# Attention and SwiGLU FFN on one core: a reordered ramp, a set FFN pace, and batch 1 loaded in natural layout

## The chip, the core, the metric

The kernel runs on one core of a Trainium2 chip. Times are device microseconds (us). A profile is one profiled execution; its span is a little shorter than the timed run. One slot is the work on one pair of heads; a batch has four. TensorE is called PE, VectorE DVE, ScalarE ACT, GpSimd POOL, SyncE SP. In the views, `st` and `X` are the PSUM banks (the memory that matmuls write) of scores and of values, `f` those of the FFN and of transposes, `PT` the exponentials, `XN` the attention output, `XS` and `XT` its normalized copy before and after transposition. The granted clock is the share of TensorE's full clock: 1.00 is full, 0.50 half.

## The reference

Block-causal attention over q, k, v of shape (8 batches, 8 heads, 576 tokens, 64), blocks of 64; its output is laid out as 4608 tokens of 512, and a gated FFN follows:

```python
scores = q @ k.T / 8;  scores = where(block_i >= block_j, scores, -1e9)
x = softmax(scores) @ v                       # -> x[b * 576 + s, h * 64 + d]
xn = x / sqrt(mean(x * x) + 1e-6) * rms_g
out = (silu(xn @ w_gate) * (xn @ w_val)) @ w_out      # 512 -> 1536 -> 512
```

## The kernel before

All loads are issued by POOL, which casts float32 to bfloat16 on the way. Batches 0 and 1 are loaded "wide": six tokens to a partition, so one run in memory is 1536 B, and TensorE transposes them. Batches 2 to 7 are loaded in natural layout (256 B runs) and transposed by DMA.

```python
def load_wide(b, n, h0, h1):                   # 96 partitions, 6 tokens of 64 each
    pool_dma(out=wide[b][:, n, hs, :, :]..., in_=(q, k)[n][b, hs, :, :].rearrange("h (p s) d -> p h (s d)", s=SLOT))
def load_qk_head(b, h):                        # natural: two loads for each head
    pool_dma(out=t[:, hp, kb:kb + NC, ds], in_=k[b, h, 0:TAIL, :].rearrange("(c p) d -> p c d", p=P))
    pool_dma(out=t[:, hp, 0:NC, ds], in_=q[b, h, 0:TAIL, :]...)
def prep(b, hp):                               # DMA transpose, issued by SP
    sp(nc.sync.dma_start_transpose(out=T, in_=QKN[b % 2][:, hp, :, :]))
```

A slot is made of pieces: three score groups of the current pair (each followed by an exp on ACT) and two values groups of the previous pair (probabilities times V, then an eviction on DVE into `XN`). After each piece a share of the queued FFN work runs, so that PE has something to do while ACT works. FFN work is counted in units of one 512-wide matmul; gate, value and down groups are 4 units each. A chunk of tokens joins the queue when its attention is done and normalized: `norm_squares` on ACT, a reciprocal root in small DVE steps, `XS` on DVE, transposes on PE, `XT` on ACT.

```python
for n in range(3):
    pieces.append(cur.scores(n))
    if n < 2: pieces.append(prev.values(n))
...
fast = b == 0
at(norms, s0, norm_squares(b));  at(norms, s0 + (0 if fast else 1), norm_scale(b))
s1 = s0 + (1 if fast else 2);    at(norms, s1, xt_by_pe(b)); at(rels, s1, release(b))
...
budget = max(0, total - RESERVE) / (nxt - s)   # units for this slot
```

(Shortened. In slot 4, the first of batch 1, this kernel already puts both values pieces ahead of the scores.)

The softmax here doesn't subtract the row's maximum and nothing guards it: scores larger than these inputs give would overflow.

Of the kernel before, what the change touches and what calls it, by code (L numbers as in the profile page):

```python
# [11 lines left out]
BF16 = mybir.dt.bfloat16  # L12
AF = mybir.ActivationFunctionType
# [4 lines left out]
def kernel(  # L18
# [11 lines left out]
    nc = tc.nc  # L30
# [19 lines left out]
    const = ctx.enter_context(tc.tile_pool(name="const", bufs=1))  # L50
    tp = ctx.enter_context(tc.tile_pool(name="tp", bufs=3))
    xtp = ctx.enter_context(tc.tile_pool(name="xtp", bufs=3))
# [27 lines left out]
    def pool(ins):  # L80
        return chain("POOL", ins)
# [18 lines left out]
    PTS = [const.tile([P, PTW], BF16, name=f"PT{i}") for i in range(2)]  # L100
    QK0 = [const.tile([P, 2, S], BF16, name=f"QK0{i}") for i in range(2 * HP)]
    ident = const.tile([P, P], BF16, name="ident")
# [4 lines left out]
    wide = []  # L107
    for b in range(2):
        t = hbuf.tile([P, NMC, BANK], BF16, name="HT")
        wide.append(t[0:PQ, :, :].rearrange("p m q -> p (m q)")[:, 0:2 * H * SLOT * D].rearrange(  # L110
            "p (n h s d) -> p n h s d", n=2, h=H, s=SLOT))
    WIDE = 2

# [58 lines left out]
    def tpose_wide(b, hp):  # L172
        T = QK0[b * HP + hp]
        for n in range(2):
            t = fbank().bitcast(BF16)
            for s in range(SLOT):
                for par in range(2):
                    pe(nc.tensor.transpose(t[par * D:(par + 1) * D, s * PQ:(s + 1) * PQ],
                                           wide[b][:, n, 2 * hp + par, s, :],
                                           ident[0:PQ, 0:PQ]))  # L180
            nc.vector.tensor_copy(out=T[:, n, :].rearrange("p (j s) -> p j s", s=SLOT),
                                  in_=t[:, 0:S].rearrange("p (s j) -> p j s", s=SLOT))
        tposed[b, hp] = T[:, 0, :], T[:, 1, :]
# [21 lines left out]
    class Pair:  # L205
# [18 lines left out]
        def scores(self, n, split=None):  # L224
# [3 lines left out]
            end = 0  # L228
            tail = self.full and n == 2
            for c, lo, w, o in self.groups[n]:  # L230
# [6 lines left out]
            if tail:  # L237
                for h in range(2):
                    self.qk(XB[h][:, BANK - BLK:BANK], h, NC, TAIL, BLK)
                    self.col[h, NC, NC] = 3 * T4 + h * BLK  # L240
            if split:
# [11 lines left out]
            if tail:  # L253
                for h in range(2):
                    a = 3 * T4 + h * BLK
                    nc.scalar.activation(out=PT[:, a:a + BLK], in_=XB[h][:, BANK - BLK:BANK],
                                         func=AF.Exp, scale=SM_SCALE)
            for tn, o, step, cnt in self.diags:
# [63 lines left out]
    def norm_scale(b, tiles):  # L322
        XN = xn_tiles[b]
        n = len(tiles)
        XS = xs.tile([P, n, DM], BF16, name="XS")

        def root():
            norm_tiles[b, tiles[0], "rs"] = inv_sqrt(norm_tiles.pop((b, tiles[0])), n)
            norm_tiles[b, tiles[0]] = XS

        def one(j, t):
            rs = norm_tiles[b, tiles[0], "rs"]
            nc.vector.tensor_scalar(out=XS[:, j, :], in0=XN[:, t, :],  # L333
                                    scalar1=rs[:, j:j + 1], scalar2=None, op0=ALU.mult)
        return [root] + [lambda j=j, t=t: one(j, t) for j, t in enumerate(tiles)]
# [49 lines left out]
    def up_gate(i, k):  # L385
        pg, _ = up_tile(i, k)
        th = act.tile([P, BANK], FP32, name="th")
        nc.scalar.activation(out=th, in_=pg, func=AF.Tanh, scale=0.5)  # L388
        nc.vector.scalar_tensor_tensor(out=th, in0=th, scalar=1.0, in1=pg,  # L389
                                       op0=ALU.add, op1=ALU.mult)  # L390
        gates[i, k] = th

    def up_val(i, k):
        pv, ht = up_tile(i, k)
        nc.vector.tensor_tensor(out=ht, in0=gates.pop((i, k)), in1=pv, op=ALU.mult)  # L395

    outs = {}

    def down(i, s, part):
# [6 lines left out]
        if part == 2:  # L406
# [3 lines left out]
            sp(nc.sync.dma_start(out=out[r0:r0 + P, :], in_=ob))  # L410

    def add_chunk(i):
        n = (chunks[i][1] - chunks[i][0]) // P
        for k in range(NMC * n // 4):
            queue.append((4, lambda k=k: up_gate(i, k)))
            queue.append((4, lambda k=k: up_val(i, k)))
        for s in range(n):
            for part in range(3):
                queue.append((4, lambda s=s, part=part: down(i, s, part)))

# [9 lines left out]


    load_wide(0, 0, 0, 2)
    load_wide(0, 1, 0, 2)
    make_identity(nc, ident)
    load_wide(0, 0, 2, 4)
    load_wide(0, 1, 2, 4)
    load_v_chunk(0, 0)
    load_v_chunk(0, 1)
    load_wide(0, 0, 4, H)
    load_wide(0, 1, 4, H)  # L440
    load_v_chunk(0, 2)
# [9 lines left out]
    for m in range(0, NMC, 3):  # L451
        load_up_weights(m, m + 3)
    for n in range(2):
        load_wide(1, n, 0, H)
    for c in range(NC):
# [7 lines left out]
    early = [Pair(0, hp, EARLY) for hp in range(HP)]  # L463
    for hp in range(HP):
        tpose_wide(0, hp)
        early[hp].scores(0, (None, FB[0:2], FB[2:4])[hp % 3])
        if hp > 1:
            early[hp - 2].values(0)
    early[2].values(0)
    early[3].values(0)  # L470
    clear_v(1)
# [18 lines left out]
    for b in range(B):  # L490
        tiles = T1 if b == 0 else TA
        s0 = index[b, HP - 1] + 1
        fast = b == 0
        at(norms, s0, lambda b=b, tiles=tiles: norm_squares(b, tiles))
# [5 lines left out]
    e0 = index[1, 0]  # L500
    mids = {e0 + i: lambda i=i: tpose_wide(1, i + 1) for i in range(HP - 1)}
    for b in range(WIDE, B):
        for hp in range(HP):
            at(preps, index[b, hp] - 2, lambda b=b, hp=hp: prep(b, hp))
    for b in range(WIDE, B):
        s0 = max(index[b - 2, HP - 1] - 1, e0)
        s1 = index[b, 0] - 2
        if b > WIDE:
            at(loads, s0, lambda b=b: load_qk_tail(b))
            for h in range(H):  # L510
                at(loads, s0 + h * (s1 - s0) // H, lambda b=b, h=h: load_qk_head(b, h))
# [4 lines left out]

    RESERVE = 12
    prev = None
    for s, sl in enumerate(slots):
        todo = [g for f in norms.pop(s, []) for g in f()]  # L520
        nxt = min([r for r in ready if r > s] + [999])
        total = sum(c for c, _ in queue)
        budget = max(0, total - RESERVE) / (nxt - s) if nxt < 999 else total / (len(slots) - s)
        cur = None
# [7 lines left out]
        for n in range(3):  # L532
            pieces.append((lambda n=n: cur.scores(n)) if cur else None)
            if n < 2:
                pieces.append((lambda n=n: prev.values(n)) if prev else None)
        if s == e0:
            tpose_wide(1, 0)
            pieces = [pieces[1], pieces[3], pieces[0], pieces[2], pieces[4]]
        left = 0
        for i, f in enumerate(pieces):  # L540
            if f:
                f()
            if i == 2 and s in mids:
                mids[s]()
            if i == 3 and s > e0:
# [40 lines left out]
```

## Time and profile before

| | before |
|---|---|
| median of the first 3 runs | 414.1 us |
| profiled span | 412.1 us |
| PE busy | 379.6 us (92%) |
| PE idle in 0 to 100 us, in 100 to 380, after | 26.0, 2.7, 3.7 us |
| time of a batch once PE is full | 41.78 us |

The table says where to look: PE is full after the first quarter, so every step is judged by when the ramp ends and whether the full stretch stays full. The lines are in the prediction below.

### The profile page before, as it was taken

The page shows a single profiled execution, that of the slowest core. Times are in us where ns is not written, and L with a number is a line of the kernel's source. Part 1 is how long each engine was busy: PE and PEld are TensorE (multiplying, and loading weights), DVE is VectorE, ACT ScalarE, POOL GpSimd, SP SyncE. Part 2 cuts the span into 40 slices and gives each one's busy share as a digit, 9 for nine tenths or more (in the row PEclk, how much of TensorE's full clock was granted, in tenths as well). Part 3 has the DMA queues.
Part 4 walks back from the last instruction along what each step waited for, and adds up shares of the span by engine and source line. Part 5 has one row for each costly group of instructions (what it writes and reads, how often), then busy time and mean ns, then how long its engine had stood idle before and what let it go on. Part 6 is the DMA issues. An engine that isn't in the chain of part 4 may idle for free.

```text
span 412.1 us, 7988 instructions
## 1 busy us (share of the span) xinstructions
PE 379.6 (92%) x3096; PEld 193.4 (47%) x3096; DVE 249.4 (61%) x652; ACT 235.5 (57%) x451; POOL 134.0 (33%) x184
## 2 busy tenths in 40 slices
PE   3469779887999999999999999999999999999996
PEld 2337545664444544454445444544454444444442
DVE  5455864673779276926692669267926872752760
ACT  2276756786585758576757575757674625322321
POOL 8643497886079006910691060000000000000000
PEclk9999998999999999999999999999999999999999
DMA  9999999999299639972998397231020002002002
GB/s 99 190 203 186 169 89 169 131 149 130 61 107 117 105 76 102 110 128 68 83 125 130 70 79 69 86 81 35 0 78 27 0 27 76 1 2 102 1 2 102
DMA packets 140950, 36.70 MB, mean 89 GB/s; under 512 B 127600, under 2 KB 136304, under 8 KB 140912
## 3 DMA queue, kind: packets, MB, share of 16 engines
q0 software_dynamic: 103712, 18.89, 56.8%
q1 hardware_dynamic: 37200, 17.31, 18.4%
q8 instruction: 24, 0.39, 0.4%
q14 instruction: 14, 0.11, 0.1%
HBM read 37.75 MB, written 9.44 MB: 115 GB/s over the span
## 4 chain that ended last, share of the span: by engine, by line
PE 75%; DVE 12%; ACT 7%; DMA 2%; issue 2%; POOL 1%; ACTq 0%; POOLq 0%; DVEq 0%
PE f_91 L87 19%; PE f_89 L87 15%; PE f_88 L87 15%; PE f_90 L87 12%; PE st L87 6%; PE X_86 L87 3%; PE X_87 L87 3%; DVE HT L395 2%; DVE th L389 2%; DVE XS L333 2%; DMA HT<-in_k_dram 2%; ACT th L388 2%; DVE XN L284 2%; ACT sq L318 2%; ACT PT_96 L246 1%
## 5 line engine op out<-in xcount | busy, mean ns | idle before, releaser
L87 PEld LDWEIGHTS <-WV 128*128 128x128 bf16 x480 | 43.5, 98 | 45.9 <-issue 6.9
L87 PEld LDWEIGHTS <-WG 128*128 128x128 bf16 x480 | 43.5, 98 | 42.9 <-issue 4.3
L87 PEld LDWEIGHTS <-HT 128*128 128x128 bf16 x432 | 38.6, 98 | 47.3 <-issue 9.6
L389 DVE SCALAR_TENSOR_TENSOR th<-th,f_88 128x512 f32<-128x512 f32 x53 | 36.4, 686 | 40.3 <-ACT th L388 39.9
L87 PE MATMUL f_90<-XT,WG 128*128 128x512 bf16 (+1 forms) x248 | 56.7, 356 | 0.0
L87 PE MATMUL f_91<-XT,WV 128*128 128x512 bf16 (+1 forms) x240 | 55.7, 358 | 0.0
L87 PE MATMUL f_89<-XT,WV 128*128 128x512 bf16 (+1 forms) x240 | 55.7, 358 | 0.0
L87 PE MATMUL f_88<-XT,WG 128*128 128x512 bf16 (+1 forms) x232 | 55.4, 366 | 0.0
L388 ACT ACTIVATE th<-f_88 128x512 f32<-128x512 f32 x53 | 31.9, 603 | 40.3 <-PE f_88 L87 39.2
L246 ACT ACTIVATE PT_96<-st 128x1024 bf16<-128x1024 f32 x44 | 45.1, 1024 | 16.2 <-PE st L87 16.2
L246 ACT ACTIVATE PT_97<-st 128x1024 bf16<-128x1024 f32 x44 | 45.7, 1038 | 11.4 <-PE X_87 L87 6.6
L87 PE MATMUL f_91<-WO,HT 128*128 128x512 bf16 x192 | 48.2, 384 | 2.1 <-ACT ob L408 2.1
L389 DVE SCALAR_TENSOR_TENSOR th<-th,f_90 128x512 f32<-128x512 f32 x55 | 37.7, 686 | 19.0 <-ACT th L388 18.9
L388 ACT ACTIVATE th<-f_90 128x512 f32<-128x512 f32 x55 | 33.1, 601 | 27.6 <-PE f_90 L87 24.6
L395 DVE TENSOR_TENSOR HT<-th,f_89 128x512 bf16<-128x512 f32 x54 | 37.1, 687 | 5.6 <-PE f_89 L87 1.6
L395 DVE TENSOR_TENSOR HT<-th,f_91 128x512 bf16<-128x512 f32 x54 | 37.1, 686 | 3.6
L78 POOL DMA_DIRECT2D VN_95<-in_v_dram x20 | 17.1, 874 | 51.6 <-PE X_87 L87 45.7
L87 PE MATMUL st<-QKT 64*128 64x512 bf16 (+4 forms) x240 | 28.2, 297 | 2.2 <-ACT PT_97 L246 1.6
L78 POOL DMA_DIRECT2D VN_94<-in_v_dram x20 | 17.1, 906 | 36.6 <-PE X_87 L87 36.6
L87 PE MATMUL f_88<-WO,HT 128*128 128x512 bf16 x108 | 26.2, 380 | 0.2 <-DVE HT L395 0.2
L78 POOL DMA_DIRECT2D QKN_92<-in_k_dram x30 | 23.0, 766 | 8.9 <-DMA QKT<-QKN_92 3.4
L318 ACT ACTIVATE sq<-XN 128x512 bf16<-128x512 f32 x40 | 25.6, 639 | 0.1
(126 smaller groups left out, 475.5 us busy)
## 6 DMA issues: line engine op xcount, KB each, us to landing
out_dram<-ob SPq DMA_DIRECT2D x36, 256.0 KB, 2.0
VN_94<-in_v_dram POOLq DMA_DIRECT2D x16, 128.0 KB, 4.8
VN_95<-in_v_dram POOLq DMA_DIRECT2D x16, 128.0 KB, 4.7
WG<-in_moe_w_gate_dram POOLq DMA_DIRECT2D x4, 384.0 KB, 10.8
WV<-in_moe_w_val_dram POOLq DMA_DIRECT2D x4, 384.0 KB, 11.7
WO<-in_moe_w_out_dram POOLq DMA_DIRECT2D x2, 768.0 KB, 14.0
QKN_92<-in_k_dram POOLq DMA_DIRECT2D x24, 64.0 KB, 3.5
QKN_92<-in_q_dram POOLq DMA_DIRECT2D x24, 64.0 KB, 3.6
```

The costliest lines, as they stand in the source:

```text
L78: return chain("POOL", nc.gpsimd.dma_start(**kw))
L87: pe(nc.tensor.matmul(dst, w, r, start=start, stop=stop))
L246: nc.scalar.activation(out=PT[:, a0:a0 + T4], in_=ST, func=AF.Exp, scale=SM_SCALE)
L284: nc.vector.tensor_tensor(out=xn_tiles[self.b][:, t0:t0 + n, f0:f0 + m * D].rearrange("p t (h d) -> p h t d", h=m), in0=xv[:, :, :, 0:D], ...
L318: nc.scalar.activation(out=sq, in_=XN[:, t, :], func=AF.Square, accum_out=ss[:, j:j + 1])
L333: nc.vector.tensor_scalar(out=XS[:, j, :], in0=XN[:, t, :], scalar1=rs[:, j:j + 1], scalar2=None, op0=ALU.mult)
L388: nc.scalar.activation(out=th, in_=pg, func=AF.Tanh, scale=0.5)
L389: nc.vector.scalar_tensor_tensor(out=th, in0=th, scalar=1.0, in1=pg, op0=ALU.add, op1=ALU.mult)
L395: nc.vector.tensor_tensor(out=ht, in0=gates.pop((i, k)), in1=pv, op=ALU.mult)
```

## The change

The intent is to shorten the ramp. Q and K of batch 0 are loaded ahead of its V and the transposes of all its pairs are issued together; the FFN units of slots 2 to 9 are set by a table; batch 1 is loaded and transposed as later batches are, which spares TensorE 96 transposes. Around this, the pieces are reordered, the last small score block of both heads shares one PSUM bank, batch 1 is normalized one slot earlier, some DVE instructions get a fixed order, and chunk 0's down groups wait for chunk 1. Smaller edits come along that no run takes apart: the identity matrix is built in place, `tp` has a fourth buffer, and slot 4 loses its own order. The diff is shortened and reworded to fit.

```diff
+            copy = nc.scalar.copy if b == 0 and n == 1 else nc.vector.tensor_copy   # tpose_wide
-            tail = self.full and n == 2       # both heads, banks X0 and X1
+            tail = self.full and n > 0        # head 1 at n=1, head 0 at n=2, both in bank X0
-            nc.vector.tensor_scalar(out=XS...        # and th, HT
+            chain("DVE", nc.vector.tensor_scalar(out=XS...
+    later = []                                # down groups of chunk 0 wait for chunk 1
-    load_v_chunk(0, 0); load_v_chunk(0, 1)    # then Q, K of heads 4 to 7
+    for h in range(4, H, 2): load_wide(0, 0, h, h + 2); load_wide(0, 1, h, h + 2)
+    load_v_chunk(0, 0); load_v_chunk(0, 1)
-    for n in range(2): load_wide(1, n, 0, H)
+    load_qk_tail(1)
+    for h in range(H): load_qk_head(1, h)
-        tpose_wide(0, hp); early[hp].scores(0, ...); early[hp - 2].values(0)   # in turn
+    tpose_wide(0, 0); tpose_wide(0, 1); early[0].scores(0); tpose_wide(0, 2) ...
+    for pr in early: pr.values(0)
-        fast = b == 0
+        fast = b < 2
+    PACE = {2: 24, 3: 24, 4: 12, 5: 12, 6: 12, 7: 12, 8: 22, 9: 22}
-            pieces.append(scores(n)); if n < 2: pieces.append(values(n))
+            if n < 2: pieces.append(values(n)); pieces.append(scores(n))
```

More of the change, by code (lines that the diff above doesn't have):

```diff
@@ L6 @@
 from concourse import bass_utils, mybir
-from concourse.masks import make_identity
 from concourse._compat import with_exitstack
@@ L50 @@
     const = ctx.enter_context(tc.tile_pool(name="const", bufs=1))
-    tp = ctx.enter_context(tc.tile_pool(name="tp", bufs=3))
+    tp = ctx.enter_context(tc.tile_pool(name="tp", bufs=4))
     xtp = ctx.enter_context(tc.tile_pool(name="xtp", bufs=3))
@@ L100 @@
     PTS = [const.tile([P, PTW], BF16, name=f"PT{i}") for i in range(2)]
-    QK0 = [const.tile([P, 2, S], BF16, name=f"QK0{i}") for i in range(2 * HP)]
+    QK0 = [const.tile([P, 2, S], BF16, name=f"QK0{i}") for i in range(HP)]
     ident = const.tile([P, P], BF16, name="ident")
@@ L107 @@
     wide = []
-    for b in range(2):
-        t = hbuf.tile([P, NMC, BANK], BF16, name="HT")
-        wide.append(t[0:PQ, :, :].rearrange("p m q -> p (m q)")[:, 0:2 * H * SLOT * D].rearrange(
+    wide.append(hbuf.tile([P, NMC, BANK], BF16, name="HT")[0:PQ, :, :].rearrange(
+        "p m q -> p (m q)")[:, 0:2 * H * SLOT * D].rearrange(
             "p (n h s d) -> p n h s d", n=2, h=H, s=SLOT))
-    WIDE = 2
+    WIDE = 1
     def load_wide(b, n, h0, h1):
@@ L180, in tpose_wide @@
                                            ident[0:PQ, 0:PQ]))
-            nc.vector.tensor_copy(out=T[:, n, :].rearrange("p (j s) -> p j s", s=SLOT),
-                                  in_=t[:, 0:S].rearrange("p (s j) -> p j s", s=SLOT))
+            copy = nc.scalar.copy if b == 0 and n == 1 else nc.vector.tensor_copy
+            copy(out=T[:, n, :].rearrange("p (j s) -> p j s", s=SLOT),
+                 in_=t[:, 0:S].rearrange("p (s j) -> p j s", s=SLOT))
         tposed[b, hp] = T[:, 0, :], T[:, 1, :]
@@ L237, in scores @@
             if tail:
-                for h in range(2):
-                    self.qk(XB[h][:, BANK - BLK:BANK], h, NC, TAIL, BLK)
-                    self.col[h, NC, NC] = 3 * T4 + h * BLK
+                h = 2 - n
+                o = BANK - (2 - h) * BLK
+                self.qk(XB[0][:, o:o + BLK], h, NC, TAIL, BLK)
+                self.col[h, NC, NC] = 3 * T4 + h * BLK
             if split:
@@ L253, in scores @@
             if tail:
-                for h in range(2):
-                    a = 3 * T4 + h * BLK
-                    nc.scalar.activation(out=PT[:, a:a + BLK], in_=XB[h][:, BANK - BLK:BANK],
-                                         func=AF.Exp, scale=SM_SCALE)
+                nc.scalar.activation(out=PT[:, 3 * T4 + h * BLK:3 * T4 + (h + 1) * BLK],
+                                     in_=XB[0][:, o:o + BLK], func=AF.Exp, scale=SM_SCALE)
             for tn, o, step, cnt in self.diags:
@@ L332, in one @@
             rs = norm_tiles[b, tiles[0], "rs"]
-            nc.vector.tensor_scalar(out=XS[:, j, :], in0=XN[:, t, :],
-                                    scalar1=rs[:, j:j + 1], scalar2=None, op0=ALU.mult)
+            chain("DVE", nc.vector.tensor_scalar(out=XS[:, j, :], in0=XN[:, t, :],
+                                                 scalar1=rs[:, j:j + 1], scalar2=None,
+                                                 op0=ALU.mult))
         return [root] + [lambda j=j, t=t: one(j, t) for j, t in enumerate(tiles)]
@@ L388, in up_gate @@
         nc.scalar.activation(out=th, in_=pg, func=AF.Tanh, scale=0.5)
-        nc.vector.scalar_tensor_tensor(out=th, in0=th, scalar=1.0, in1=pg,
-                                       op0=ALU.add, op1=ALU.mult)
+        chain("DVE", nc.vector.scalar_tensor_tensor(out=th, in0=th, scalar=1.0, in1=pg,
+                                                    op0=ALU.add, op1=ALU.mult))
         gates[i, k] = th
@@ L394, in up_val @@
         pv, ht = up_tile(i, k)
-        nc.vector.tensor_tensor(out=ht, in0=gates.pop((i, k)), in1=pv, op=ALU.mult)
+        chain("DVE", nc.vector.tensor_tensor(out=ht, in0=gates.pop((i, k)), in1=pv,
+                                             op=ALU.mult))
     outs = {}
@@ L418, in add_chunk @@
             for part in range(3):
-                queue.append((4, lambda s=s, part=part: down(i, s, part)))
+                later.append((4, lambda s=s, part=part: down(i, s, part)))
+        if i > 0:
+            queue.extend(later)
+            later.clear()
     def ffn(cost):
@@ L429, in ffn @@
         return cost - done
+    nc.vector.memset(ident, 0.0)
     load_wide(0, 0, 0, 2)
     load_wide(0, 1, 0, 2)
-    make_identity(nc, ident)
     load_wide(0, 0, 2, 4)
+    pool(nc.gpsimd.affine_select(out=ident, in_=ident, compare_op=ALU.not_equal, fill=1.0,
+                                 base=0, pattern=[[-1, P]], channel_multiplier=1))
     load_wide(0, 1, 2, 4)
+    for h in range(4, H, 2):
+        load_wide(0, 0, h, h + 2)
+        load_wide(0, 1, h, h + 2)
     load_v_chunk(0, 0)
     load_v_chunk(0, 1)
-    load_wide(0, 0, 4, H)
-    load_wide(0, 1, 4, H)
     load_v_chunk(0, 2)
@@ L452 @@
         load_up_weights(m, m + 3)
-    for n in range(2):
-        load_wide(1, n, 0, H)
+    load_qk_tail(1)
+    for h in range(H):
+        load_qk_head(1, h)
     for c in range(NC):
@@ L463 @@
     early = [Pair(0, hp, EARLY) for hp in range(HP)]
-    for hp in range(HP):
-        tpose_wide(0, hp)
-        early[hp].scores(0, (None, FB[0:2], FB[2:4])[hp % 3])
-        if hp > 1:
-            early[hp - 2].values(0)
-    early[2].values(0)
-    early[3].values(0)
+    tpose_wide(0, 0)
+    tpose_wide(0, 1)
+    early[0].scores(0)
+    tpose_wide(0, 2)
+    early[1].scores(0, XB)
+    tpose_wide(0, 3)
+    early[2].scores(0)
+    early[3].scores(0, FB[0:2])
+    for pr in early:
+        pr.values(0)
     clear_v(1)
@@ L500 @@
     e0 = index[1, 0]
-    mids = {e0 + i: lambda i=i: tpose_wide(1, i + 1) for i in range(HP - 1)}
     for b in range(WIDE, B):
@@ L504 @@
             at(preps, index[b, hp] - 2, lambda b=b, hp=hp: prep(b, hp))
-    for b in range(WIDE, B):
+    for b in range(2, B):
         s0 = max(index[b - 2, HP - 1] - 1, e0)
         s1 = index[b, 0] - 2
-        if b > WIDE:
+        if b > 2:
             at(loads, s0, lambda b=b: load_qk_tail(b))
@@ L522 @@
         total = sum(c for c, _ in queue)
-        budget = max(0, total - RESERVE) / (nxt - s) if nxt < 999 else total / (len(slots) - s)
+        budget = PACE[s] if s in PACE else max(0, total - RESERVE) / (nxt - s) if nxt < 999 else total / (len(slots) - s)
         cur = None
@@ L532 @@
         for n in range(3):
-            pieces.append((lambda n=n: cur.scores(n)) if cur else None)
             if n < 2:
                 pieces.append((lambda n=n: prev.values(n)) if prev else None)
-        if s == e0:
-            tpose_wide(1, 0)
-            pieces = [pieces[1], pieces[3], pieces[0], pieces[2], pieces[4]]
+            pieces.append((lambda n=n: cur.scores(n)) if cur else None)
         left = 0
@@ L542 @@
                 f()
-            if i == 2 and s in mids:
-                mids[s]()
             if i == 3 and s > e0:
```

## The prediction

> **What bounds the kernel now.** I read the page first, by slices of 10.3 us.
>
> ```profile
> span 412.1 us, 7988 instructions
> PE 379.6 (92%) x3096; PEld 193.4 (47%) x3096; DVE 249.4 (61%) x652; ACT 235.5 (57%) x451; POOL 134.0 (33%) x184
> ...
> PE   3469779887999999999999999999999999999996
> ...
> ACT  2276756786585758576757575757674625322321
> ...
> DMA  9999999999299639972998397231020002002002
> ```
>
> TensorE is full from about 100 us on. Only the first ten slices have holes, and there the DMA engines are busy too. So a change can gain only in the ramp, or by taking work off TensorE. The view of stretches (columns: length; busy us of PE, PEld, DVE, ACT, POOL; granted clock; DMA; GB/s) shows how much:
>
> ```profile
> 15.00:20.00 5.00, 3.37 (x50) 2.40 (x50) 2.69 (x7) 1.58 (x3) 3.12 (x5) 1.00 1.33 203
> 20.00:25.00 5.00, 2.03 (x17) 1.01 (x17) 1.80 (x7) 3.11 (x8) 2.44 (x3) 1.00 1.32 202
> ...
> 55.00:60.00 5.00, 2.88 (x25) 1.32 (x22) 3.67 (x11) 2.04 (x7) 5.00 (x8) 1.00 1.37 86
> 60.00:65.00 5.00, 4.36 (x40) 2.36 (x41) 0.25 (x2) 3.33 (x8) 5.00 (x8) 0.66 1.56 145
> ...
> 140.00:200.00 60.00, 59.27 (x479) 28.16 (x478) 38.75 (x99) 38.22 (x72) 20.53 (x28) 1.00 0.75 90
> ```
>
> PE is busy 74.0 us of the first 100 (my sum of all such rows), so 26.0 of the 32.5 us that it idles in the whole span lie there; 2.7 lie in 100 to 380 us and 3.7 in the tail. Then I followed the ramp in the timeline:
>
> ```profile
> 13.82 0.69 PE L178 MATMUL f_89<-ident,HT 96*64 96x96 bf16 x12 [0.91 <-DMA HT<-in_k_dram]
> ...
> 21.30 0.61 PE L87 MATMUL st<-QK_98 64*128 64x320 bf16 x4
> ...
> 51.02 0.39 PE L87 MATMUL st<-QK_103 64*128 64x512 bf16 x2 [1.59 <-ACT PT_96 L246]
> ...
> 58.80 0.19 PE L87 MATMUL X_87<-QK_103 64*128 64x64 bf16 x1 [2.08 <-DVE XN L284]
> ```
>
> The last queries and keys of batch 0 arrive at 13.8; the early part of batch 0 ends and slot 0 (a slot is one pair of heads) starts at 21.30. Later PE waits for single results of ACT and DVE because there is too little FFN work to put between. The first score matmuls of slots 1, 2, 6, 8, 10 and 11 stand at 25.73, 30.36, 61.57, 75.41, 88.45 and 98.22 us; from there on a batch takes 41.8 us and is pure PE work. The result is therefore read at slot 11: when it starts, and how much FFN work is done by then.
>
> **What the Trainium skill says.** "TensorE: Matmul & The Clock Gate", Part 1 (The HAM clock gate), says that TensorE runs at half clock until it has been active for a while and falls back when idle. The trace agrees: a group of eight 256-wide matmuls takes 1.82 us at 30.96 and 0.98 at 36.31, and the clock reads 0.66 after the 2.08 us wait. Part 4 of that page (PE-mode transpose) says that a TensorE transpose lands in PSUM and needs a copy; here 12 of them take 0.45 us warm and each copy 0.75 us on DVE. "DMA: Bandwidth & Descriptors", Specifications, asks for at least 512 B per transfer for line rate. The trace agrees: batch 1's wide K (1536 B read per run) landed 576 KB in 3.7 us and its Q in about 2.5, whereas V (256 B runs) took about 0.9 us per 128 KB, 190 against 145 GB/s written. The same page, section "Issuing engines are not separate DMA queues", has all queues on the same 16 engines; DMA transposes beside loads needed 3.3 to 9.0 us (median 4.8) from issue to landing.
>
> **The change, part by part.**
>
> Batch 1 layout: 96 transposes of the 3096 matmuls go, 8 groups of 12, about 0.3 us of PE each (42.67 to 42.95 start to start), 2.4 us; with them 8 DVE copies of 0.75 us, 6.0 us, in the stretch 43 to 66 us. In their place come 18 more loads from POOL at about 0.74 us each, 13 us of issue, and 4 DMA transposes. POOL keeps eight loads in flight: each issue waits for the landing eight earlier. The last up-weights landed near 31.7 us, so the natural loads start flowing there: heads 0 and 1 land near 35 us, the rest is issued at 0.74 us each until 41.4, V of batch 1 until 45.8 (landing near 49), the down-weights then land near 55 rather than 45 and 49. The first transposed pair is due at 35 plus 5 to 9, at 40 to 44 us.
>
> Early part: all Q/K loads now precede V, every load is two heads, the K copies go to ACT. The eighth load need not wait for 2 x 128 KB of V (about 2 us), so it lands near 12 instead of 13.8. PE no longer interleaves values with transposes. Walking the chain: last K transposes done 12.6, its copy on ACT behind an exp 13.3, scores 13.9, four values groups of 0.5 us, two of which wait for the eviction of their bank (about 0.7 us): slot 0 starts at about 16.4. Gain here 4.9 us.
>
> Slots 0 and 1: the pieces of a slot now begin with the values of the previous pair, ahead of its first scores. With no FFN work yet, these 24 matmuls (1.5 us at half clock, 26.27 in the timeline) leave the shadow of an exp and stand in the chain, after exp and memset. Slot 1's scores start at 22.5, slot 2's values at 27.3, the first gate group (1.8 us, still cold) ends at 30.6 and the scores behind it at 31.1. Before, the same work was done at 33.9. Of 4.9 us, 2.8 are left.
>
> Slots 2 and 3 at pace 24 run all 12 up-groups of chunk 0 (48 units; a unit is one 512-wide matmul, 0.216 us) against 8 before. Eleven more at 0.93 us, and 2.5 us of attention, end at 43.8.
>
> Slots 4 and 5 have no FFN work at all: the queue is empty, the down-groups of chunk 0 now wait for chunk 1, and chunk 1 is released at the end of slot 5, so pace 12 has no effect there. They run on the exp chain, about 1.76 us per score group (82.07 to 83.83 in the timeline), with three squares in slot 4: slot 5 scores at 50.4, its last at 54.0. Then come exp, tail and four XT evictions of 0.68 us on ACT, the first gate group behind them, and only then the scores of slot 6: 59.0.
>
> Slots 6 and 7 (three groups each) take 11.9 us together on the same chain, to 70.9. Slots 8 and 9 at pace 22, with six groups each, are PE work: 7.9 us, and 9.3 with batch 1's norm transposes, which come one slot earlier than before. Slot 10 with eight groups of 0.87 us ends at 97.8.
>
> Sum: slot 11 starts at 97.8 instead of 98.22, with 152 units done instead of 132: 0.4 + 20 x 0.216 = 4.7 us. After that PE work is the same: 28 full pairs have the same matmuls; only the order of pieces and the tail bank differ. Values now follow the last scores after two FFN groups, 1.73 us, while exp, tail exp and memset need about 1.5, so no new stall is due in most slots; the tail no longer waits for the DVE eviction of bank X_87 (0.4 to 0.5 us in some ramp slots), but may cost as much elsewhere.
>
> **Rivals.**
>
> 1. The whole hole closes. The step from slot 5's to slot 6's first scores takes 8.6 us above (50.4 to 59.0), against about 5.3 for three bare score groups of 1.76. If PE reorders or the evictions are quicker than I have them, some 3 of those go, and with the full 4.9 us of the early part kept, another 2: gain about 10 us, 404. For it: the pace table looks tuned, and DVE loses 6 us of copies in that stretch. Against: nothing fills slots 4 and 5.
> 2. The natural loads become the bound. V of batch 1 lands near 49 and slot 5 begins with its values at about 49.8; the transposed pair is due at 40 to 44 and needed at 44.7. With POOL fully busy from 50 to 65 us already before, a slip of 3 us passes straight through: 412 to 413.
> 3. New stalls in every steady slot because values follow exp more closely: 0.2 us in 22 slots would be 4 us and cancel the gain, 413 to 414. Margin 0.2 us by the numbers above, so possible.
> 4. The gain is hidden anyway, because FFN work is limited by what attention releases: against it, three chunks of FFN remain after the last pair (323 to 408 us is PE alone), so any unit done earlier shortens the end.
>
> **Range and chances.** The sum gives 409.4; I shade it to 408.5 since rival 1 looks a little likelier than 2 and 3 together. The parts are uncertain by about 1 us for the early part, 2 for slots 4 to 6 (clock falling to half in the thin stretch included), 2 for the loads, 2 for the steady slots, together about 3.6: range 403 to 413. Two per cent faster means under 405.8, some 0.75 of that spread below the middle: 0.25. Slower by two per cent needs 422: 0.02.
>
> **What would show it.** Slot 0 scores near 16.4; chunk 0's 12 up-groups done by 44; PE mostly idle at 45 to 57, waiting for ACT; score groups of slot 6 near 59; slot 11 near 98 with five FFN groups more behind it than before; 3000 matmuls; batch period still 41.8 us. I am wrong if slot 4 or 5 waits for a DMA by more than 2 us, if the batch period moves by over 0.5 us, or if slots 4 to 6 take much less than the 15 us from 43.8 to 59.0.

## The result

The changed kernel took **427.09 us** (median, 423.80 to 428.23, four runs) against 414.31 us of the kernel before in the same session. The ratio is **1.0297**, 95% interval 1.0237 to 1.0358. A ratio here is the mean time of one kernel's fast runs over that of the other's of the same rounds, so it is not quite the ratio of the medians quoted. The change made the kernel 3% slower; I had forecast 408.5 us within 403 to 413.

The page of the changed kernel, the same lines as before, with the granted clock:

```profile
span 425.3 us, 7791 instructions
PE 381.7 (90%) x2956; PEld 196.4 (46%) x3000; DVE 237.5 (56%) x641; ACT 238.5 (56%) x455; POOL 148.3 (35%) x203
...
PE   3689448879999999999999999999999999999996
...
PEclk9999757998999999999999999999999999999999
DMA  8999999999999944996698469141011002002002
```

The work went down as forecast: 3000 weight loads against 3096. Yet PE is no less busy, 381.7 against 379.6 us, because matmuls took longer: the clock row drops to 7, 5 and 7 in the fifth to seventh slice. (The 44 matmuls fewer than weight loads are records missing from the trace.) The view of stretches (length; busy us of PE, PEld, DVE, ACT, POOL; clock; DMA; GB/s) shows the hole:

```profile
40.00:50.00 10.00, 6.02 (x72) 4.16 (x69) 4.65 (x13) 7.05 (x14) 8.50 (x11) 0.93 2.51 132
50.00:60.00 10.00, 3.25 (x34) 2.18 (x36) 1.44 (x10) 1.51 (x3) 3.34 (x5) 0.50 1.73 159
60.00:70.00 10.00, 8.50 (x75) 5.53 (x72) 5.59 (x22) 6.23 (x14) 4.67 (x7) 0.55 1.24 119
...
120.00:140.00 20.00, 18.84 (x153) 9.05 (x153) 16.10 (x43) 13.37 (x28) 14.47 (x20) 1.00 1.32 104
```

From 50 to 60 us no engine is busy for more than 34% of the time. From 60 to 70 PE is 85% busy, but at a clock of 0.55, so it does about half of that. In the last row 1.16 us of PE are missing; before, the same stretch was full:

```profile
120.00:140.00 20.00, 20.00 (x172) 9.93 (x170) 14.44 (x43) 13.71 (x28) 13.18 (x19) 1.00 1.37 127
```

The timeline names the waits (start, length, instruction, in brackets the idle time before it and its releaser):

```profile
16.47 0.61 PE L86 MATMUL st<-QK_98 64*128 64x320 bf16 x4
...
45.05 0.39 PE L86 MATMUL st<-QKT 64*128 64x512 bf16 x2
...
50.46 0.27 PE L86 MATMUL X_86<-VN_95,PT_96 128*128 128x65 bf16 x2 [1.87 <-DMA VN_95<-in_v_dram]
...
57.98 0.22 PE L86 MATMUL X_86<-VN_95,PT_96 128*128 128x65 bf16 x1 [2.68 <-DMA VN_95<-in_v_dram]
58.13 0.61 PE L86 MATMUL st<-QKT 64*128 64x512 bf16 x2
...
94.31 0.23 PE L345 MATMUL f_90<-ident,XS 128*128 128x128 bf16 x1 [1.25 <-DVE XS L331]
...
103.67 0.39 PE L86 MATMUL st<-QKT 64*128 64x512 bf16 x2
```

The ramp starts as forecast (slot 0 at 16.47, slot 4's first scores at 45.05, where 44.7 was forecast). Then the values of slot 5 wait five times for V of batch 1, together 8.0 us, and since they now stand ahead of that slot's scores, the scores wait too. At 94.31 PE meets the norm transposes of batch 1 while DVE is still making XS. Set against the steps of the prediction:

| event | predicted | measured | slip in this step |
|---|---|---|---|
| slot 0, first scores | 16.4 | 16.47 | 0.1 |
| end of slot 3 | 43.8 | 43.80 | 0 |
| slot 5, first scores | 50.4 | 58.13 | 7.7 |
| slot 6, first scores | 59.0 | 66.94 | 0.2 |
| slot 8 begins | 70.9 | 79.31 | 0.5 |
| slot 9 begins | 78.8 | 87.65 | 0.4 |
| slot 10 begins | 88.1 | 101.40 | 4.4 |
| slot 11 begins | 97.8 | 110.72 | -0.4 |
| slot 11 to the end | 309.6 | 314.6 | 5.0 |

A slot begins with its first piece; slots 5 and 6 are given by their first scores, as in the prediction. The 309.6 is 412.1 - 98.22 of the kernel before, less 20 units of 0.216 us. The slips add to 17.9; less the gain of 4.7 forecast this is 13.2 us, the difference of the spans.

### The profile page after: what moved, and what is told of

Read it like the earlier page. It is cut to its first block, busy times and chain, and to the rows that moved or that the text cites. A ratio compares the mean times of both kernels' runs of the same rounds, so it can differ in the third digit from the quotient of the medians.

```text
span 425.3 us, 7791 instructions
## 1 busy us (share of the span) xinstructions
PE 381.7 (90%) x2956; PEld 196.4 (46%) x3000; DVE 237.5 (56%) x641; ACT 238.5 (56%) x455; POOL 148.3 (35%) x203
## 4 chain that ended last, share of the span: by engine, by line
PE 67%; ACT 10%; DMA 8%; DVE 7%; POOL 5%; issue 2%; ACTq 0%; POOLq 0%; DVEq 0%
PE f_91 L86 16%; PE f_89 L86 14%; PE f_88 L86 14%; PE f_90 L86 11%; PE st L86 5%; DMA WV<-in_moe_w_val_dram 4%; ACT sq L316 3%; PE X_87 L86 3%; DMA VN_95<-in_v_dram 3%; ACT PT_96 L246 3%; PE X_86 L86 3%; POOL QKN_93 L77 2%; ACT th L387 2%; DVE HT L394 2%; DVE th L388 2%
## 5 line engine op out<-in xcount | busy, mean ns | idle before, releaser
L246 ACT ACTIVATE PT_97<-st 128x1024 bf16<-128x1024 f32 x44 | 44.9, 1021 | 37.2 <-PE st L86 20.3
L246 ACT ACTIVATE PT_96<-st 128x1024 bf16<-128x1024 f32 x44 | 45.0, 1022 | 30.8 <-PE st L86 19.4
L388 DVE SCALAR_TENSOR_TENSOR th<-th,f_90 128x512 f32<-128x512 f32 x54 | 37.1, 687 | 12.3 <-ACT th L387 11.7
L86 PE MATMUL f_91<-WO,HT 128*128 128x512 bf16 x160 | 40.3, 379 | 1.3 <-ACT ob L408 0.5
L86 PE MATMUL st<-QKT 64*128 64x512 bf16 (+1 forms) x280 | 34.0, 305 | 7.1 <-ACT PT_96 L246 4.0
L86 PEld LDWEIGHTS <-QKT 64*128 64x128 bf16 x336 | 15.1, 95 | 43.7 <-issue 39.2
L77 POOL DMA_DIRECT2D QKN_93<-in_k_dram x40 | 30.8, 770 | 8.0 <-DMA WG<-in_moe_w_gate_dram 5.2
L77 POOL DMA_DIRECT2D QKN_93<-in_q_dram x40 | 30.8, 771 | 7.5 <-DMA WV<-in_moe_w_val_dram 5.0
L77 POOL DMA_DIRECT2D VN_95<-in_v_dram x20 | 17.3, 915 | 45.4 <-PE X_87 L86 45.4
L260 DVE MEMSET PT_96<- 64x64 uint32 (+1 forms) x62 | 6.5, 114 | 41.9 <-ACT PT_96 L246 39.5
## 6 DMA issues: line engine op xcount, KB each, us to landing
WV<-in_moe_w_val_dram POOLq DMA_DIRECT2D x4, 384.0 KB, 12.3
```

The costliest lines, as they stand in the source:

```text
L77: return chain("POOL", nc.gpsimd.dma_start(**kw))
L86: pe(nc.tensor.matmul(dst, w, r, start=start, stop=stop))
L246: nc.scalar.activation(out=PT[:, a0:a0 + T4], in_=ST, func=AF.Exp, scale=SM_SCALE)
L260: nc.vector.memset(blk[:, :, 0:BLK], 0.0)
L388: chain("DVE", nc.vector.scalar_tensor_tensor(out=th, in0=th, scalar=1.0, in1=pg, op0=ALU.add, op1=ALU.mult))
```

## The experiments

Three places slipped: late V in slot 5, the norm in slot 9, and the full stretch. The theory was that each has one part of the change behind it: the natural layout, the early norm, the order of pieces. The main rivals were that DMA capacity only moves the wait, and that the set pace, the fixed DVE order or the deferred down groups are at fault. All 16 runs gave correct results. The first eight were timed in three rounds, the last eight in five; all ratios use fast runs, while the medians quoted are over all runs. Two runs are compared by their ratios, times 414.5 us; such a difference is uncertain by 1 to 4 us (from the two intervals), and where that covers it the text says so.

### One part of the changed kernel undone

**V of batch 1 ahead of its Q and K.**

```diff
+    for c in range(NC): load_v_chunk(1, c)
+    load_v_tail(1)
     load_qk_tail(1)
     for h in range(H): load_qk_head(1, h)
```

> The changed kernel with one edit: V of batch 1 is loaded before Q and K of batch 1. Theory (late V): the 8 us in which the values of slot 5 waited for V between 48.6 and 58.0 us go, so do some of the half-clock matmuls after it; slot 5 scores near 50, time 417 to 420 us. Rival (DMA capacity): the wait only moves to the transposed Q and K of batch 1, slot 4 or 5 scores wait for them by 5 us or more, and the time stays at 424 or more.

Measured 425.07 us, ratio to before 1.0209 (1.0141 to 1.0277), 0.9% or about 3.6 us below the changed kernel's ratio, which is within the two intervals. The wait did go: slot 5's scores start at 50.8. But slots 6, 8 and 10 start at 61.0, 77.0 and 101.9, against 66.9, 81.3 and 103.7 in the changed kernel, so 7.4 us of lead shrink to 1.8. Slot 6 now waits 1.41 us for its transposed pair, and slot 9 alone takes 16.7 us. The theory got the wait right and its worth wrong; the rival is right in part.

**Scores ahead of values again.**

```diff
-            if n < 2: pieces.append(values(n))
             pieces.append(scores(n))
+            if n < 2: pieces.append(values(n))
```

> The changed kernel with one edit: in each slot the first scores stand before the previous pair's values again, as before the change. Theory (values too close behind exp): the PE waits on exp tail and memset after 112 us go, about 5 us; slot 5's first scores no longer stand behind the late V either, so its exps run during the wait: 418 to 422 us. Rival (the steady waits come from the fixed DVE order or from the tail in one bank): within 1.5 us of the changed kernel, 425 or more.

Measured 422.15 us, ratio 1.0171 (1.0126 to 1.0216), 5.2 us better. The gain came in the ramp (slot 10's scores at 96.3 instead of 103.7, a part of it only because they now come first in their slot). The full stretch hardly healed: batches take 42.12, 42.34 and 41.76 us, since the tail block, which the change moved to n=1 in the bank of the values just written, now waits for their eviction (2.8 us in 112 to 335 us).

**Batch 1 wide again.** The edit puts back the two wide loads, the transposes on TensorE in slots 4 to 6 and their buffers.

> The changed kernel with batch 1 loaded wide and transposed on TensorE again; everything else as changed. Theory (the natural layout makes V late): V of batch 1 lands by about 42 us, the 8 us wait goes, 96 transposes of about 2.4 us return: 419 to 422 us. Rival (the wait comes from the earlier ramp or from the down-weights, not from the layout): a wait of 5 us or more stays in slots 4 to 6, 425 or more.

Measured 423.96 us, ratio 1.0220 (1.0192 to 1.0248), 3.2 us better, and short of the 419 to 422 expected; slot 5 starts at 52.0 without a wait for V, which lands by 41.4. As with V first, slot 9 takes the lead back: 84.5 to 100.6.

### One part of the change alone

**Early part alone, on the kernel before** (load order, K copies on ACT, transposes ahead, values at the end).

> The kernel before with only the early part changed (Q and K of batch 0 loaded ahead of V two heads at a time, K copies on ACT, transposes of all pairs ahead, values at the end). Theory: slot 0 starts near 16.4 instead of 21.3 and most of the 4.9 us lasts, less about 3 us of waiting for the down-weights, which land at 45 and 49 us: 409 to 412 us. Rival (the ramp's start is hidden by later loads): 413.5 to 415 us.

Measured **409.59 us**, ratio **0.9885** (0.9848 to 0.9923): this version beats both kernels. Slot 4's scores start at 39.8 against 45.2, 5.4 us earlier, and 4.8 us (1.15% of 414) last to the end. Its page:

```profile
span 406.7 us, 7941 instructions
...
PE   3689778779999999999999999999999999999996
...
PEclk9999999989999999999999999999999999999999
```

The second and third slices are 6 and 8 instead of 4 and 6: that is the shorter early part. The tenth is 9 instead of 7, as the ramp ends sooner. The clock is full but for one slice. Slots 4 and 5 still have FFN work here, and batch 1 still comes wide.

**Order of pieces alone, on the kernel before.**

> The kernel before with only the order of pieces changed (values of the previous pair ahead of the first scores, tail as before). Theory (the order leaves values waiting for exp and memset): batch period 42.3 instead of 41.78 us, 1.5 us lost in each of slots 1 and 2, together 4 to 6 us: 418 to 420 us. Rival (the order costs nothing; the longer period comes from the tail's single bank or from the fixed DVE order): 413 to 416 us, period 41.8.

Measured 418.66 us, ratio 1.0125 (1.0076 to 1.0174): 5.2 us lost. Slot 4 starts at 48.5 instead of 45.2, and batches take 42.39 us instead of 41.78. Its waits of PE from 112 to 335 us (waiter, releaser: us in all, times, longest):

```profile
PE X L87 <- DVE PT L262: 2.0, 6, 0.4
PE f L87 <- ACT ob L408: 0.9, 5, 0.2
```

X is the values' bank and L262 the memset after the exp. In the kernel before, that line isn't there; only the second kind is, with 1.6 us. The order alone makes values wait for the end of exp, tail and memset. The rival, the shared tail bank or the DVE order, isn't needed for it: this kernel has neither.

### Parts undone together

**V first, pace spread over slots 2 to 5.**

```diff
-    PACE = {2: 24, 3: 24, 4: 12, ...
+    PACE = {2: 12, 3: 12, 4: 12, ...
```

> The changed kernel with V of batch 1 ahead of its Q and K (as in the first experiment) and the pace of slots 2 and 3 cut from 24 to 12, so that chunk 0's 48 units are spread over slots 2 to 5. Theory (pace 24 empties slots 4 and 5, and the clock gate then halves TensorE for 17 us): no half-clock stretch between 45 and 65 us, first scores of slot 6 near 54 instead of 61, 415 to 418 us. Rival (the half clock comes from DMA waits, not from missing FFN work): the stretch stays and the time is 422 or more.

Measured 425.81 us, ratio 1.0241 (1.0179 to 1.0303), no better than V first alone. Slot 4's scores now waited 2.67 us for their transposed pair and still began at 44.8: the time saved by fewer groups in slots 2 and 3 ran into the natural load. Expectation missed; the half clock came right behind that wait (matmuls of 0.61 us from 46.9 where 0.39 is the full-clock time), as the rival had it.

**The same, with the norm of batch 1 one slot later.**

```diff
-        fast = b < 2
+        fast = b == 0
```

> As the run before it in this list (V first, pace spread), and the norm of batch 1 put back one slot later (scale in slot 9, transposes in slot 10). Theory (the early norm makes PE wait 4 to 7 us for XS in slot 9, as the chain on ACT and DVE is not done): slot 9 takes about 9 us instead of 14 to 17, 3 to 5 us less than the run before it, 411 to 414 us. Rival (the chain's wait only moves into slot 10): within 1.5 us of the run before it.

Measured 418.12 us, ratio 1.0102 (1.0054 to 1.0150): 5.8 us better than the run before it. Slot 9 takes 8.2 us (85.7 to 93.9) instead of 15.8. The gain over the run before is as large as expected or larger, the time itself missed its 411 to 414, and it is the first sign that the early norm is the largest part.

**The same, with the old order and tail banks.**

> The changed kernel with V first, pace spread, norm one slot later, and the old order of pieces and old tail banks. What stays of the change is the early part, the natural layout of batch 1, the fixed DVE order and the deferred down-groups. Theory (the natural layout itself is worth its 96 transposes once V is not late): batch period 41.8, 406 to 410 us, at or below the kernel before with the early part alone (409.6). Rival (18 more loads and 4 DMA transposes cost more than they save): 412 or more.

Measured 416.84 us, ratio 1.0066 (1.0041 to 1.0091). The rival holds: what stays of the natural layout costs more than its transposes. The timeline at slot 4:

```profile
46.09 0.60 PE L86 MATMUL st<-QKT 64*128 64x512 bf16 x2 [9.49 <-DMA QKT<-QKN]
```

Now that the ramp is faster, PE is ready for batch 1 at 36.6 us and its transposed Q and K, loaded behind V here, come at 46. In the changed kernel they landed at 40.0, and the long slots 2 and 3 (to 43.8) hid that.

### One factor on a good base

The base is the run above with batch 1 wide. It keeps the early part, the deferred down groups and the fixed DVE order, and also, which the expectation below does not list, the pace table (12 in slots 2 to 7, 22 in 8 and 9) and the smaller edits.

> The all-back kernel of the list before (pace spread, norm one slot later, old order of pieces, old tail banks), with batch 1 loaded wide and transposed on TensorE again, and V behind it as before the change. What stays of the change: early part, deferred down-groups, fixed DVE order. Theory (the natural layout comes too late for slot 4 when the ramp is faster: 9.5 us of waiting for the DMA transpose there): no DMA wait over 2 us in slots 4 and 5, 407 to 411 us, as the kernel before with the early part alone (409.6). Rival (the deferred down-groups or the fixed DVE order cost the time): 414 or more.

Measured 413.94 us, ratio 0.9978 (0.9959 to 0.9997). Not the 407 to 411 expected: something in what stays costs 4 us against the early part alone. The base is sound for comparing, so the next three change one thing each, in the same session. Its profiled run was the fastest of its 22 (411.48 us).

**Pace 24 in slots 2 and 3.**

> The wide base with only the pace of slots 2 and 3 set to 24 again. Theory (pace 24 leaves slots 4 and 5 empty and the clock gate halves TensorE there): a half-clock stretch of 10 us or more between 42 and 65 us, 3 to 7 us slower than the wide base. Rival (pace is neutral, the half clock came from the late loads): within 1.5 us of the wide base, no stretch over 4 us.

Measured 414.09 us, ratio 0.9976 (0.9959 to 0.9993): no difference. The half-clock stretch is there all the same (the base's profile has a shorter one, with 0.83 in each of the first two of these rows):

```profile
40.00:50.00 10.00, 6.49 (x109) 4.45 (x107) 6.32 (x15) 5.84 (x12) 3.86 (x6) 0.81 1.46 188
50.00:60.00 10.00, 6.16 (x75) 4.10 (x72) 7.01 (x25) 4.95 (x12) 10.00 (x15) 0.50 1.60 134
60.00:70.00 10.00, 8.60 (x111) 6.12 (x110) 5.00 (x13) 6.52 (x13) 7.18 (x11) 0.83 2.53 134
```

So the theory was right about the clock and wrong about the time. What half clock costs by itself is not separated here: the same edit also does units earlier, which may make up for it. The record speaks against calling it free. Of the base's 22 runs, all of one program, the 13 with a mean clock under 0.986 took 414.5 us on average and the other 9 took 412.7. This is a correlation, no test; in the kernel with pace 24 there is no such trend.

**Norm of batch 1 one slot earlier.**

> The wide base with only the norm of batch 1 one slot earlier, as in the change. Theory (PE meets the transposes before XS is ready): waits for XS of 3 us or more in slot 9, 2 to 5 us slower than the wide base. Rival (earlier norm feeds the FFN queue earlier and pays): equal or faster than the wide base.

Measured 422.63 us, ratio 1.0184 (1.0156 to 1.0212): 8.5 us lost by this line alone, more than any other part. Slot 9 takes 16.7 us (80.1 to 96.8) against 8.4 in the base. PE waits for XS five times, 4.4 us in all, beginning with

```profile
87.95 0.23 PE L347 MATMUL f<-ident,XS 128*128 128x128 bf16 x1 [2.58 <-DVE XS L333]
```

and the record of the clock has half speed for 6.8 us (88.8 to 95.6). The chain behind it, in the changed kernel's timeline (last eviction of batch 1, first square, start of the root, XS):

```profile
83.91 0.49 DVE L282 TENSOR_TENSOR XN<-X_87,rd 128x320 f32<-128x320 f32 x1
85.49 0.64 ACT L316 ACTIVATE sq<-XN 128x512 bf16<-128x512 f32 x1
...
90.64 0.17 DVE L292 TENSOR_SCALAR x<-ss 128x5 f32<-128x5 f32 x1 [0.76 <-ACT sq L316]
...
93.77 2.32 DVE L331 TENSOR_SCALAR XS<-XN,y 128x512 bf16<-128x512 f32 x5
```

It runs from 83.9 to 96.1 us: 12.2 us, longer than the slot of 8 to 9 us that it is given. It is serial and shares ACT and DVE with exps and gates.

**Natural layout, Q and K ahead of V as in the change.**

> The wide base with only the layout of batch 1 changed: natural, with DMA transposes, Q and K ahead of V as in the change. Theory (natural layout is late): slot 4's scores wait for the transposed pair by 3 to 6 us, slot 5's values for V until 50 us or later; 6 to 10 us slower than the wide base. Rival (the layout only loses where V is ahead of it, and saves 2.4 us of transposes): within 2 us of the wide base.

Measured 418.90 us, ratio 1.0073 (1.0046 to 1.0100): 3.9 us lost, less than expected, with a wide scatter (414.7 to 420.0 us in the fast runs; two runs of 421.2 and 425.1 us count as slow). Both waits are there:

```profile
40.38 0.61 PE L86 MATMUL st<-QKT 64*128 64x512 bf16 x2 [3.84 <-DMA QKT<-QKN]
...
56.97 0.21 PE L86 MATMUL X<-VN,PT 128*128 128x65 bf16 x1 [2.16 <-DMA VN<-in_v_dram]
```

V of batch 1 is complete only near 57 us, as in the changed kernel (58), although the pieces are in the old order. So the late V belongs to the layout.

### What was left open

**The base without the fixed DVE order.**

```diff
-        chain("DVE", nc.vector.scalar_tensor_tensor(out=th, ...))      # and XS, HT
+        nc.vector.scalar_tensor_tensor(out=th, ...)
```

> The wide base without the fixed order of XS, gate and value instructions on DVE. Theory (the fixed order puts three XS, a value and a gate instruction ahead of the eviction that the tail waits for: 3.4 us of PE waiting in slot 5): that wait falls under 1.5 us, 2 to 4 us faster than the wide base, 410 to 412 us. Rival (the deferred down-groups are the loss): within 1 us of the wide base.

Measured 411.82 us, ratio 0.9927 (0.9900 to 0.9954), 2.1 us better than the base. In the base, slot 5's tail block waited

```profile
54.59 0.21 PE L86 MATMUL X<-QK 64*128 64x64 bf16 x1 [3.40 <-DVE XN L284]
```

since three XS, one value and one gate instruction stood on DVE between the reciprocal (51.42) and the eviction (54.05) of that bank. Without the fixed order the same block waits under half as long:

```profile
53.77 0.19 PE L86 MATMUL X<-QK 64*128 64x64 bf16 x1 [1.49 <-DVE XN L284]
```

What is left against the early part alone is 1.7 us, within the intervals.

**The base with the down groups not deferred.**

> The wide base with the down-groups of chunk 0 queued at once, not deferred behind chunk 1. Rival theory (deferring leaves fewer units for slots 4 and 5): 2 to 4 us faster than the wide base. Theory of the fixed DVE order: within 1 us of the wide base, since the pace and not the queue sets the units of slots 2 to 5.

Measured 415.09 us, ratio 1.0005 (0.9981 to 1.0029): about 1 us slower than the base, within the intervals. Deferring isn't the loss.

**Early part alone, plus the early norm.**

> The kernel with the early part alone, plus only the norm of batch 1 one slot earlier; DVE order free. Theory (the chain from the last values of batch 1 over squares, root and XS takes about 12 us, longer than a slot, so PE waits whatever the DVE order): 3 to 8 us slower than the early part alone (409.6), 413 to 418 us. Rival (early norm hurts only with the fixed DVE order): 408 to 411 us.

Measured 415.56 us, ratio 1.0013 (0.9996 to 1.0031) against 0.9885 without it: 5.3 us lost with DVE free to order. The first norm transposes waited 4.17 us for XS. The early norm costs by itself; under the fixed order it cost 8.5.

**The changed kernel without the fixed DVE order.**

> The changed kernel without the fixed order on DVE, everything else as changed. Theory (fixed order is a small part beside late V, order of pieces and early norm): 0 to 4 us faster than the changed kernel, 423 to 427 us. Rival (the fixed order is what makes the early norm and the tail waits costly): 420 or less.

Measured 425.64 us, ratio 1.0269 (1.0224 to 1.0314), 1.2 us better than the changed kernel, within the intervals. It is a small part there.

### The parts side by side

| part | measured by | us (ratio difference times 414.5) |
|---|---|---|
| early part | alone on before | -4.8 |
| order of pieces | alone on before; undone in the change | +5.2; +5.2 |
| early norm of batch 1 | on the early part; on the base; undone with V first and pace 12 | +5.3; +8.5; +5.8 |
| natural layout of batch 1 | on the base; undone in the change | +3.9; +3.2 |
| fixed DVE order | undone in the base; in the change | +2.1; +1.2 |
| pace 24 in slots 2 and 3 | on the base | 0 |
| deferred down groups | undone in the base | -1.1 |

With the smaller figure of each they sum to 9.0 us, with the larger to 13.8; the change lost 12.3 (2.97%). They don't add exactly: a wait taken out in slot 5 was often given back in slot 9. The figures for the deferred groups and for the fixed order in the change are not clear of noise. Not tested at all: the pace table against the old budget rule (only 24 against 12 in two slots), the tail bank by itself, and the smaller edits.

## Why the prediction was wrong

**What held.** The early part: 4.9 us of gain, slot 0 at 16.4; measured 16.47, and 4.8 us as a kernel of its own. The loss in slots 1 and 2 by the order (slot 1's scores at 22.5, measured 22.58), the end of slot 3, the empty slots 4 and 5, the step of 8.6 us from slot 5 to slot 6 (measured 8.8), slot 8: all within 0.5 us. The 96 transposes less. The step from slot 5 to slot 6 may be right partly by luck: PE ran it at half clock (0.50 from 58 to 68 us), which the sum did not contain. Two of the prediction's own signs of being wrong came true: slot 5 waited for a DMA by 8.0 us, and the batch period moved by 0.56 us. Two of its readings are slightly off, without effect on the sum: in the timeline the groups of eight take 1.89 and 1.05 us (at 30.90 and 36.25), and batch 1's Q and K landed 2.75 and 3.77 us after the load before them, about 181 GB/s and not 190.

**The step that failed first** is "V of batch 1 until 45.8 (landing near 49)". Issue was right: the five loads were issued from 41.94 to about 46. The landing was 58: 8.4 to 12.5 us after issue, where I had put about 3, as short as natural Q and K loads from 49 us on in the kernel before (2.6 to 4.4). I told the transposes' own latency under load, not what loads in company take. Before, V had landed 11 to 17 us after issue too, but it was issued from 21.9 us on, far ahead. Rival 2 had this wait, with a slip of 3 us; it was 7.7. That four DMA transposes and the down-weights share the engines with V in that stretch is seen; how much each of them delays it was not separated. The engines moved 56 GB/s in 46 to 48 us, against 173 in the two us before, with two of the transposes in flight; but with V first they moved 130 and 204 GB/s in 46 to 48 and 48 to 50 us, beside transposes too. So why V lands late stays open; that it does so with the natural layout, and not with the wide one, is shown.

**The second** is "9.3 with batch 1's norm transposes, which come one slot earlier than before". I counted the transposes as PE work and never walked the chain that feeds them, though the kernel before shows all its durations. It takes 12.2 us; slot 9 took 13.75 where 9.3 was forecast, with 2.2 us of waits for XS and then a clock of 0.57 in 96 to 100 us. Shown by two kernels that change only this line. It was in no rival.

**The third** is "Values now follow the last scores after two FFN groups, 1.73 us, while exp, tail exp and memset need about 1.5, so no new stall is due in most slots". A margin of 0.2 us is no margin when ACT and DVE have other work in front: batches took 42.34 us instead of 41.78, about 0.14 us a slot. From 112 to 335 us the values waited 3.1 us for exp, tail exp and memset. The order alone, on the kernel before, gives 42.39. Rival 3, in kind, with 0.2 us in 22 slots, and right in size. I gave it too little weight.

**Half clock.** I put "clock falling to half in the thin stretch included" into the spread. It fell for about 20 us. What that cost is not separated: in the pace experiment a stretch of about 17 us, against about 7 in the base's profile, went with the same time, but with units done earlier.

**Why they came together.** The prediction was a sum of gains, with the rivals as alternatives. They weren't alternatives: the natural layout, the order and the early norm each cost on its own, so 2 and 3 both came true.

## What to carry to other kernels

When work is moved one slot earlier, walk the chain that feeds it and compare its length with the slot, not only the work itself with the engine that does it. A consumer that stood behind other work had slack you cannot see in the profile; moving it to the front spends that slack in every iteration. Before replacing a few large loads in a ramp by many small ones with a second DMA pass, ask when the last dependent load is issued and what will share the engines with it, and try the parts of a bundled change one at a time: here one of them was worth 1.15% and the others buried it.

## What the Trainium skill lacked or had wrong

- "TensorE: Matmul & The Clock Gate", Part 1 (HAM oscillation): its rule speaks of idle gaps over about 3.4 us. In the base with pace 24 no wait of PE listed between 44 and 64 us is longer than 1.82 us, with PE busy 6.16 of 10 us, and the clock still stood at 0.50 through 50 to 60 us. In the changed kernel it read 0.63 in 48 to 50 us, with waits of at most 1.2 us between 45.05 and 48.6 us and PE busy 0.42 us of 46 to 48. So thin work came with half clock without such a gap. The next section, "A second HAM failure mode", does tell of short idles in one kernel, but not how long they were.
- The same section counts half of the throttled time as extra time. Pace 24 lowered the mean clock of the runs from 0.986 to 0.979, about 5 us more at half clock (my estimate from clock and time), so about 2.7 us more by that count (an estimate from the page); measured were 414.09 against 413.94 us. This does not refute the count, as the edit also moved work; the section has no case where other waits hide the slow matmuls.
- "DMA: Bandwidth & Descriptors", "Anatomy of one DMA": its fit of a fixed 2 us plus bytes over the fabric rate says nothing of loads in company. In the changed kernel V loads of 128 KB took 8.4 to 10.3 us, the last one of 64 KB 12.5 us, from issue to landing, with DMA transposes and down-weights in flight.
- No page gives what one more DMA transpose costs its neighbours. Here four of them landed 4.7 to 14.9 us after issue beside the loads; what they cost the loads was not separated here either.
